# Threshold attention and a feed-forward block: where chunks are converted, when q and k are asked for, and where a slot's products end

## The chip, the cores and the metric

The kernel runs on one core of one Trainium2 chip. The time is the device time of one execution in microseconds (us). A core has five engines that run their own instruction streams and wait for each other by semaphores: TensorE (PE; its weight loads are listed apart as PEld), VectorE (DVE), ScalarE (ACT), GpSimd (POOL) and SyncE (SP), which here only issues DMAs.

## The reference

Eight batches of eight heads with 576 rows of 64 features go through an attention that keeps only the scores within tau of the row's maximum. The heads' outputs side by side are the input x (512 features) of a block with layer norm, a product to 2048 hidden features, a relu, a product back, and a residual.

```python
scores = scale * np.matmul(q, k.transpose(0, 1, 3, 2))
thresh = np.max(scores, axis=-1, keepdims=True) - tau
scores = np.where(scores >= thresh, scores, -1000000000.0)
scores = scores - np.max(scores, axis=-1, keepdims=True)
attn = np.exp(scores)
attn = attn / (np.sum(attn, axis=-1, keepdims=True) + 1e-09)
attn_out = np.matmul(attn, v)                       # (8, 8, 576, 64)
x = attn_out.transpose(0, 2, 1, 3).reshape(8, 576, 512)
xn = (x - mu) / np.sqrt(var + 1e-06) * g_ln         # mu, var over the 512 features
out = x + np.maximum(xn @ w_ch1, 0.0) @ w_ch2       # 512x2048 and 2048x512
```

q, k, v and g_ln are float32. w_ch1 and w_ch2 arrive as float64, and the kernel converts them to float32 itself.

## The kernel before

The work is cut into 72 slots, nine for each batch. A slot does the scores, exponentials and thresholding of four blocks of 128 rows. Its weights are transposed and multiplied with v one slot later. In the first batch the transposing is done on TensorE (`turn_weights`); from the second on by DVE in 32x32 blocks, a way through DRAM (`scr`) and back (`em`). Between these, a slot has four places (quarters) where products of the feed-forward block are put into TensorE's stream.

```python
for n in range(NS):
    b, s = divmod(n, SLOTS)
    ticks = (0, 2, 3) if n < 6 else range(5)      # ticks of the weights' conversion
    ...
    tick(0)
    scores(b, s)                                  # PE
    run(n, -1)
    rest = exponentials()                         # DVE maxima, ACT exponentials
    es, thr = next(rest)                          # the first two blocks
    run(n, 0)                                     # asks for em of the slot before
    conversion.fetch(2)
    run_all(stores)                               # output DMAs
    second_part(n, 0)                             # products, quarter 0
    next(rest, None)                              # the last two blocks' exponentials
    u = (n + 1) // SLOTS * HP + (n + 1) % SLOTS
    if (n + 1) % SLOTS < HP and u < len(units):
        turn(u)                                   # transposes k and q of a later slot on DVE
    run_all(aside)
    tick(1)
    run(n, 1)
    second_part(n, 1)
    weights(es, thr)                              # DVE threshold, POOL normalization
    run_all(aside)
    run_all(stores)
    tick(2)
    run(n, 2)
    second_part(n, 2)
    tick(3)
    ...  # turn_weights, or turn_blocks (DVE) and four DMAs to scr
    at_quarter(n + 1, 3, lambda b=b, s=s, box=box: values_of(b, s, box[0]))
    ...
    if (n + 1) % SLOTS < HP and u + 1 < len(units):
        load_qk(u + 1)                            # eight DMAs on SyncE, into single buffers
    run_all(aside)
    conversion.fetch(2)
    run(n, 3)                                     # mean of a group, values of the slot before
    ...  # load_v
    second_part(n, 3)
    tick(4)
    run_all(aside)
```

The feed-forward block works on groups of 288 rows, two for each batch. Its products are handed out by a generator; `second_part` takes as many as a running account (`owed`) allows, by the room of each quarter.

```python
def ffn_steps(g):
    ...
    for d in range(ND):                           # 16 feature tiles of the hidden layer
        while conversion.ended < 4 * (d // 4 + 1):
            yield 0                               # weights not there yet
        p1 = ps_ff.tile([128, TOK], F32, tag="ff", name="p1")   # tag "ff": two buffers
        for c in range(NK):                       # 4 products
            product(p1, ...)
            if c < NK - 1:
                yield 1
        nc.scalar.activation(hidden[:, d], p1, func=AF.Relu)
        yield 1
        ...  # d == 1: squares; d == 8: variance (a product into "ff"), 1/std
    for m in range(NK):
        p2 = ps_ff.tile([128, TOK], F32, tag="ff", name="p2")
        for d in range(ND):
            ...
            product(p2, ..., rhs=hidden[:, d], ...)
            if d < ND - 1:
                yield 1
        aside.append(lambda m=m, p2=p2: add_to_x(g, m, p2, rb))   # DVE product o, POOL sum
        yield 1
```

The conversion turns 32 chunks of float64 words. Each takes a piece of borrowed memory for its raw words and one for what is made of them. A piece is kept with the number of the first chunk that may no longer use it, and the tick at which it was given back.

```python
def piece(self, i, wait):
    fit = [p for p in self.free if p[0] > i and p[1] < self.ticks - wait]
    if not fit:
        return None
    got = min(fit, key=lambda p: p[0])
    ...
def fetch(self, most=99):                         # DMA of raw words, got = self.piece(i, 1)
    ...
def begin(self):
    i = self.begun
    got = self.piece(i, -1)
    if got is None:
        return
    ...  # DVE: two operations into the first half; ACT: one in place, a square into the second
def carry(self):                                  # POOL: adds, gives the raw piece back
    ...
def end(self):                                    # DVE, for w_ch1 also POOL; gives the made piece back
    ...
def tick(self):
    self.ticks += 1
    if self.ended < self.carried and self.due[self.ended] <= self.ticks:
        self.end()
    if self.carried < self.begun:
        self.carry()
    if self.begun < self.fetched:
        self.begin()
```

Of the kernel before, what the change touches and what calls it, by code (L numbers as in the profile page):

```python
# [18 lines left out]
def kernel(  # L19
# [36 lines left out]
    HP = H // 2  # L56
# [6 lines left out]
    SLOTS = 2 * HP + 1  # L63
# [28 lines left out]
    units = [(b, hp) for b in range(B) for hp in range(HP)]  # L92
    loaded, values_in, turned = {}, {}, {}

    def product(out, lhsT, rhs, **flags):


        for h in range(2):
            r = slice(64 * h, 64 * h + 64)
            nc.tensor.matmul(out[r], lhsT=lhsT[:, r], rhs=rhs, **flags)  # L100
# [59 lines left out]
    class Weights:  # L160
# [67 lines left out]

        def begin(self):
            i = self.begun  # L230
            got = self.piece(i, -1)
            if got is None:
                return
            self.made[i] = got
            a, y = got[2][:, :WC], got[2][:, WC:]
            self.begun += 1
            self.due.append(self.ticks + 3)
            au, hi = a.bitcast(U32), self.words(i, U32)[:, :, 1]
            nc.vector.tensor_scalar(
                out=au, in0=hi, scalar1=3, scalar2=0x3FFFFFFF,  # L240
                op0=ALU.logical_shift_left, op1=ALU.bitwise_and,
            )
            nc.vector.scalar_tensor_tensor(
                out=au, in0=hi, scalar=0xC0000000, in1=au,
                op0=ALU.bitwise_and, op1=ALU.bitwise_or,
            )
            nc.scalar.activation(
                self.words(i, I32)[:, :, 0], self.words(i, U32)[:, :, 0],
                func=AF.Copy, scale=2.0**-29,
            )  # L250
            nc.scalar.activation(y, self.words(i, F32)[:, :, 1], func=AF.Square)
# [34 lines left out]
    def by_blocks(u):  # L286

        return units[u][0] > 0

    def turn(u):  # L290

        q_in, k_in = loaded.pop(u)
        qT = att.tile([128, 2, QH], F32, tag="qT", bufs=4, name="qT")
        kT = att.tile([128, S], F32, tag="kT", bufs=4, name="kT")
        qd = q_diag[u % HP]  # L300
        nc.gpsimd.tensor_scalar(
            out=q_in, in0=q_in, scalar1=scl_sb, scalar2=1.0, op0=ALU.mult, op1=ALU.mult
        )
        nc.vector.transpose(kT, k_in.rearrange("p n c -> p (n c)"))  # L304
        for s in range(2):
            part = q_in[:, 9 * s : 9 * s + 8]
            if by_blocks(u):
                nc.vector.transpose(
                    qT[:, s].rearrange("p (j a c) -> p a j c", j=2, a=4),
                    part.rearrange("p (a j) c -> p a j c", j=2),  # L310
                )
            else:
                nc.vector.transpose(qT[:, s], part.rearrange("p n c -> p (n c)"))
        for h in range(2):
            r = slice(64 * h, 64 * h + 64)
            nc.vector.transpose(
                qd[r, r].rearrange("p (t c) -> p t c", t=2),
                q_in[r].rearrange("p (t n) c -> p t n c", t=2)[:, :, 8],
            )
        turned[u] = (qT, kT, qd)  # L320
# [221 lines left out]
    def run_all(calls):  # L542
        now = calls[:]
        calls.clear()
        for fn in now:
            fn()
# [23 lines left out]
    def ffn_steps(g):  # L570


        xc = centred.pop(g)
        rb = None
        for d in range(ND):
            while conversion.ended < 4 * (d // 4 + 1):
                yield 0
            p1 = ps_ff.tile([128, TOK], F32, tag="ff", name="p1")
            for c in range(NK):
                product(  # L580
                    p1, lhsT=w1_sb[c][:, d * 128 : (d + 1) * 128], rhs=xc[:, c],
                    start=(c == 0), stop=(c == NK - 1),
                )
                if c < NK - 1:
                    yield 1
            nc.scalar.activation(hidden[:, d], p1, func=AF.Relu)  # L586
            yield 1
            if d == 1:
                sq = ffn.tile([128, NK, TOK], F32, tag="sq", bufs=1, name="sq")
                nc.scalar.activation(sq, xc, func=AF.Square)  # L590
                for c in range(1, NK):
                    nc.gpsimd.tensor_tensor(out=sq[:, 0], in0=sq[:, 0], in1=sq[:, c], op=ALU.add)
            if d == 8:
                var = ps_ff.tile([128, TOK], F32, tag="ff", name="var")
                product(var, lhsT=avg_sb, rhs=sq[:, 0], start=True, stop=True)
                rb = ffn.tile([128, TOK], F32, tag="rb", bufs=2, name="rb")
                nc.scalar.activation(rb, var, func=AF.Sqrt, bias=eps_sb)  # L597
                aside.append(lambda: nc.vector.reciprocal(rb, rb))  # L598
# [4 lines that stand above are left out]
                while conversion.ended < conversion.n1 + d + 1:  # L603
                    yield 0
                product(
                    p2, lhsT=w2_sb[:, d, m * 128 : (m + 1) * 128], rhs=hidden[:, d],
                    start=(d == 0), stop=(d == ND - 1),
                )
                if d < ND - 1:
                    yield 1  # L610
            aside.append(lambda m=m, p2=p2: add_to_x(g, m, p2, rb))
            yield 1

    QUARTERS = 4
# [3 lines left out]
    queue = []  # L620
    issued = 0
    owed = 0.0
# [5 lines left out]
    def run(n, i):  # L628
        for fn, args in later_calls.pop((n, i), ()):
            fn(*args)  # L630

    def ready(g):

        b, t = divmod(g, 2)
        return QUARTERS * (b * SLOTS + (HP, 2 * HP)[t] + 2) + (2, 4)[t]

    def second_part(n, i):

        nonlocal issued, owed
        if not queue:  # L640
            return
        at = QUARTERS * n + i
        g = issued // STEPS
        left = sum(ROOM[t % QUARTERS] for t in range(at, ready(g + 1))) if g + 1 < NG else 0
        owed += ((g + 1) * STEPS - issued) * ROOM[i] / left if left > 0 else 8
        while queue and owed >= 0.5:
            got = next(queue[0], None)
            if got is None:
                queue.pop(0)
                if left > ROOM[i]:  # L650
                    break
            elif got == 0:
                owed = 0.0
                break
            else:
                issued += 1
                owed -= 1
# [21 lines left out]
    for n in range(NS):  # L679
        b, s = divmod(n, SLOTS)  # L680
        ticks = (0, 2, 3) if n < 6 else range(5)

        def tick(i):
            if i in ticks:
                conversion.tick()

        tick(0)
        scores(b, s)
        run(n, -1)
        rest = exponentials()  # L690
        es, thr = next(rest)
        run(n, 0)
        conversion.fetch(2)
        run_all(stores)
        second_part(n, 0)
        next(rest, None)

        u = (n + 1) // SLOTS * HP + (n + 1) % SLOTS
        if (n + 1) % SLOTS < HP and u < len(units):
            turn(u)  # L700
        run_all(aside)
        tick(1)
        run(n, 1)
        second_part(n, 1)
        weights(es, thr)
# [6 lines that stand above are left out]
        box = []  # L712
        if by_blocks(b * HP):
            scr = turn_blocks(s, es)
            at_quarter(n + 1, 0, lambda s=s, scr=scr, box=box: box.append(fetch(s, scr)))
        else:
            made = turn_weights(s, es)
            at_quarter(n + 1, -1, next, made)
            at_quarter(n + 1, 0, lambda made=made, box=box: box.append(next(made)))
        at_quarter(n + 1, 3, lambda b=b, s=s, box=box: values_of(b, s, box[0]))  # L720
        if s in (HP, 2 * HP):
            group_ready(2 * b + (s > HP))
        if (n + 1) % SLOTS < HP and u + 1 < len(units):
            load_qk(u + 1)
        run_all(aside)
        conversion.fetch(2)
        run(n, 3)
        if b == 0 and s < HP - 2:
            load_v(s + 2)
        elif n >= SLOTS - 2 and (n + 2) % SLOTS < HP and n < NS - 2:  # L730
            load_v((n + 2) // SLOTS * HP + (n + 2) % SLOTS)
# [3 lines that stand above are left out]
# [37 lines left out]
```

## Time and profile before

| | |
|---|---|
| time, median of 3 runs | 1594.85 us (1592.58 to 1596.5) |
| span of the profiled run | 1586.6 us, 28851 instructions |
| PE busy | 1431.7 us (90%) |
| PEld busy | 854.8 us (54%) |
| DVE busy | 835.3 us (53%) |
| POOL busy | 477.1 us (30%) |
| ACT busy | 441.8 us (28%) |
| mean granted TensorE clock | 0.959 |
| DMA | 205.07 MB, mean 129 GB/s |

The page of a profile gives such sums, a picture of the span in 40 slices, and groups of like instructions by line, engine and operation. The other views are answers to questions put to the trace: who waited for whom (engine, line, what it waited for, us in total, times, longest), the busy time of each engine in a stretch, and the instructions in order of time, where the brackets at the end of a line give the engine's idle time before it and what ended that. "x5" is a count, and an arrow points from what is read to what is written. Names are those of the tiles in the kernel, with `p` for p1 and p2 and `sc` for the score banks, in which the values are summed too; lines are those of the kernel printed above.

### The profile page before, as it was taken

The page shows a single profiled execution, that of the slowest core. Times are in us where ns is not written, and L with a number is a line of the kernel's source. Part 1 is how long each engine was busy: PE and PEld are TensorE (multiplying, and loading weights), DVE is VectorE, ACT ScalarE, POOL GpSimd, SP SyncE. Part 2 cuts the span into 40 slices and gives each one's busy share as a digit, 9 for nine tenths or more (in the row PEclk, how much of TensorE's full clock was granted, in tenths as well). Part 3 has the DMA queues.
Part 4 walks back from the last instruction along what each step waited for, and adds up shares of the span by engine and source line. Part 5 has one row for each costly group of instructions (what it writes and reads, how often), then busy time and mean ns, then how long its engine had stood idle before and what let it go on. Part 6 is the DMA issues. An engine that isn't in the chain of part 4 may idle for free.

```text
span 1586.6 us, 28851 instructions
## 1 busy us (share of the span) xinstructions
PE 1431.7 (90%) x11700; PEld 854.8 (54%) x11700; DVE 835.3 (53%) x1380; ACT 441.8 (28%) x797; POOL 477.1 (30%) x737
## 2 busy tenths in 40 slices
PE   3556789999989998999989998999989999999998
PEld 2334445665555555565546555565555655565554
DVE  4856765455464555555464545555554556545210
ACT  2445542313132231313123230323223231323120
POOL 3654532222232313222232322222232322222110
PEclk7768899999999999999999999999999999999999
DMA  9610217654675556755565556745575556645300
GB/s 213 170 54 27 61 37 167 148 132 132 153 155 154 131 139 148 178 130 133 131 163 136 146 133 151 168 124 141 137 156 148 142 134 152 158 129 137 100 9 16
DMA packets 460693, 205.07 MB, mean 129 GB/s; under 512 B 275024, under 2 KB 420176, under 8 KB 460560
## 3 DMA queue, kind: packets, MB, share of 16 engines
q1 hardware_dynamic: 458160, 202.93, 52.2%
q8 instruction: 92, 1.51, 0.4%
q10 hardware_dynamic: 2368, 0.30, 0.2%
q14 instruction: 41, 0.34, 0.1%
q0 software_dynamic: 32, 0.00, 0.0%
HBM read 119.41 MB, written 83.76 MB: 128 GB/s over the span
## 4 chain that ended last, share of the span: by engine, by line
PE 64%; DVE 8%; SPq 8%; DMA 6%; issue 5%; ACT 4%; POOL 4%; POOLq 0%; ACTq 0%; DVEq 0%
PE p L100 45%; PE sc L492 9%; PE sc L359 7%; SPq L112 5%; DMA em<-scr 4%; DVE neg L372 3%; ACT e L383 3%; POOL e L395 2%; DVE e L389 2%; PE sc L100 2%; SPq L459 2%; ACT hidden L586 1%; SPq L126 1%; SPq L130 1%; DVE et L453 1%
## 5 line engine op out<-in xcount | busy, mean ns | idle before, releaser
L100 PE MATMUL p<-xc,w 128*64 128x288 f32 x4096 | 521.2, 409 | 26.3 <-ACT hidden L586 24.2
L100 PE MATMUL p<-hidden,w 128*64 128x288 f32 x4096 | 515.7, 408 | 0.0
L100 PEld LDWEIGHTS p<-xc,w 128*64 128x64 f32 x4096 | 293.5, 137 | 232.7 <-ACT hidden L586 43.8
L100 PEld LDWEIGHTS p<-hidden,w 128*64 128x64 f32 x4096 | 298.8, 138 | 192.5 <-issue 2.7
L372 DVE TENSOR_REDUCE neg<-sc 128x2 f32<-128x1152 f32 x144 | 189.4, 1353 | 315.3 <-PE sc L359 252.4
L395 POOL TENSOR_SCALAR e<-e,den 128x576 f32<-128x576 f32 x288 | 219.4, 779 | 332.8 <-DVE den L393 300.8
L383 ACT ACTIVATE e<-sc,neg 128x576 f32<-128x576 f32 x288 | 194.0, 743 | 278.4 <-DVE neg L372 278.2
L389 DVE SCALAR_TENSOR_TENSOR e<-sc,thr,e 128x576 f32<-128x576 f32 x288 | 220.0, 813 | 33.7 <-ACT e L383 33.4
L359 PE MATMUL sc<-kT,qT 64*128 64x512 f32 (+3 forms) x1024 | 161.0, 454 | 41.8 <-ACT x L509 11.6
L453 DVE STREAM_TRANSPOSE et<-e 128x1152 f32<-128x1152 f32 x112 | 153.1, 1372 | 71.7 <-POOL e L395 63.7
L586 ACT ACTIVATE hidden<-p 128x288 f32<-128x288 f32 x256 | 103.3, 414 | 253.9 <-PE p L100 253.7
L492 PE MATMUL sc<-em,v_in 128*64 128x256 f32 (+1 forms) x1536 | 154.1, 347 | 16.4 <-DMA em<-scr 11.3
L359 PEld LDWEIGHTS sc<-kT,qT 64*128 64x128 f32 x1024 | 89.4, 198 | 128.3 <-issue 79.5
L376 POOL TENSOR_SCALAR thr<-neg,low_sb 128x2 f32<-128x2 f32 x144 | 39.2, 272 | 363.9 <-DVE neg L372 362.9
L492 PEld LDWEIGHTS sc<-em,v_in 128*64 128x64 f32 x1536 | 101.9, 145 | 63.7 <-issue 19.5
L509 ACT COPY x<-sc 128x256 f32<-128x256 f32 x64 | 23.8, 372 | 355.6 <-PE sc L492 342.4
L551 POOL TENSOR_TENSOR o<-o,x 128x288 f32<-128x288 f32 x64 | 51.0, 796 | 138.8 <-DVE o L550 138.4
L550 DVE TENSOR_TENSOR o<-p,rb 128x288 f32<-128x288 f32 x64 | 28.1, 439 | 109.3 <-PE p L100 109.1
L304 DVE STREAM_TRANSPOSE kT<-k_in 128x576 f32<-128x576 f32 x32 | 24.8, 775 | 83.6 <-DMA k_in<-in_k_dram 79.7
L518 POOL TENSOR_TENSOR sum<-sum,x 128x256 f32<-128x256 f32 (+1 forms) x64 | 31.9, 498 | 104.6 <-ACT x L509 99.7
L416 PE MATMUL tp<-ident,e 128*128 128x128 f32 x144 | 26.7, 334 | 28.9 <-ACT em L423 28.5
L598 DVE RECIPROCAL rb<-rb 128x288 f32<-128x288 f32 x16 | 31.3, 1954 | 39.4 <-ACT rb L597 39.4
(93 smaller groups left out, 700.7 us busy)
## 6 DMA issues: line engine op xcount, KB each, us to landing
scr<-et SPq DMA_DIRECT2D x252, 288.0 KB, 4.9
em<-scr SPq DMA_DIRECT2D x63, 1024.0 KB, 5.9
q_in<-in_q_dram SPq DMA_DIRECT2D x128, 72.0 KB, 3.4
out_dram<-ot SPq DMA_DIRECT2D x256, 36.0 KB, 4.3
k_in<-in_k_dram SPq DMA_DIRECT2D x124, 72.0 KB, 2.6
v_in<-in_v_dram SPq DMA_DIRECT2D x64, 128.0 KB, 2.8
rest<-scr SPq DMA_DIRECT2D x63, 128.0 KB, 5.8
w<-in_moe_w_ch_dram SPq DMA_DIRECT2D x13, 512.0 KB, 4.9
```

Source lines behind the costliest of these rows:

```text
L100: nc.tensor.matmul(out[r], lhsT=lhsT[:, r], rhs=rhs, **flags)
L112: (engines[i] if engines else nc.sync).dma_start(out=t[32 * g : 32 * g + 32], in_=src[b, 2 * hp + h, :, 32 * e : 32 * e + 32].rearrange("( ...
L359: nc.tensor.matmul(sc[h][:, at : at + n], lhsT=qT[r, half, j * 128 : (j + 1) * 128], rhs=kT[r, o : o + n], start=True, stop=True,)
L372: nc.vector.tensor_reduce(out=neg[:, i], in_=sc[h][:, : 2 * S].rearrange("p (j n) -> p j n", j=2), axis=AXL.X, op=ALU.max, negate=True,)
L376: nc.gpsimd.tensor_scalar(out=thr[:, i], in0=neg[:, i], scalar1=-1.0, scalar2=low_sb, op0=ALU.mult, op1=ALU.add,)
L383: nc.scalar.activation(es[:, i], blocks[i], func=AF.Exp, bias=neg[:, i : i + 1])
L389: nc.vector.scalar_tensor_tensor(out=es[:, i], in0=blocks[i], scalar=thr[:, i : i + 1], in1=es[:, i], op0=ALU.is_ge, op1=ALU.mult, accum_o ...
L395: nc.gpsimd.tensor_scalar(out=es[:, i], in0=es[:, i], scalar1=den[:, i : i + 1], scalar2=1.0, op0=ALU.mult, op1=ALU.mult,)
L453: nc.vector.transpose(et[:, :, 64 * h : 64 * h + 64].rearrange("p n (j c) -> p j n c", j=2), es[:, 2 * h : 2 * h + 2].rearrange("p j (n c) ...
L492: nc.tensor.matmul(dst[64 * h : 64 * h + 64], lhsT=vt[:, c, h, :] if c < J else vr[:, h, :], rhs=pick(em[:, c] if c < J else er, hp, h), s ...
L551: nc.gpsimd.tensor_tensor(out=o, in0=o, in1=groups[g][:, m], op=ALU.add)
L586: nc.scalar.activation(hidden[:, d], p1, func=AF.Relu)
```

## The change

Three things change. A chunk of the conversion now takes, for what is made of its words, a piece that has been free for two ticks or more, and one just given back only if there is none. The loads of q and k are asked for right behind the turning that empties their buffers, in front of the output stores and of the writes to `scr`, where they were behind both. And in the last quarter of a slot the products go on until a feature tile of the hidden layer is complete, so that its relu can run before the next slot's exponentials.

```diff
         def begin(self):
             i = self.begun
-            got = self.piece(i, -1)
+            got = self.piece(i, 1) or self.piece(i, -1)
...
             nc.scalar.activation(hidden[:, d], p1, func=AF.Relu)
-            yield 1
+            yield 2
...
                 if d < ND - 1:
-                    yield 1
+                    yield 2
             aside.append(lambda m=m, p2=p2: add_to_x(g, m, p2, rb))
-            yield 1
+            yield 2
...
         owed += ((g + 1) * STEPS - issued) * ROOM[i] / left if left > 0 else 8
-        while queue and owed >= 0.5:
+        got = 2
+        while queue and (owed >= 0.5 or got == 1 and i == QUARTERS - 1):
             got = next(queue[0], None)
...
             turn(u)
+            if u + 1 < len(units):
+                load_qk(u + 1)
         run_all(aside)
...
-        if (n + 1) % SLOTS < HP and u + 1 < len(units):
-            load_qk(u + 1)
         run_all(aside)
         conversion.fetch(2)
```

## The prediction

> **What bounds the kernel now.** I call one pass of the outer loop a slot (n = 0 to 71), its four parts q0 to q3, and write s for n mod 9, the place in a batch. I read the busy slices first, then two stretches.
>
> ```profile
> PE   3556789999989998999989998999989999999998
> ...
> PEclk7768899999999999999999999999999999999999
> ```
>
> ```profile
> 0.00:244.70 244.70, 151.76 (x984) 93.21 (x984) 155.49 (x250) 103.21 (x180) 119.42 (x147) 0.78 0.38 96
> 244.70:1586.60 1341.90, 1279.98 (x10718) 761.54 (x10716) 679.82 (x1130) 338.57 (x617) 357.71 (x590) 0.99 0.56 135
> ```
>
> The columns are the stretch, its length, then busy PE, weight loads, DVE, ACT, POOL, then clock, DMA share and GB/s. Up to 244.7 us (slots 0 to 9, in which the weights are converted) TensorE idles 244.7 - 151.8 = 92.9 us and is granted 0.78 of its clock. Afterwards it idles 1341.9 - 1280.0 = 61.9 us in 1342. So the second stretch is bound by TensorE, and only its gaps can be won; the first is bound by something else. The waits of TensorE over the whole span say what the gaps are:
>
> ```profile
> PE tp L416 <- ACT em L423: 28.5, 13, 6.9
> PE p L100 <- ACT hidden L586: 24.2, 28, 1.5
> PE mean L100 <- DVE o L550: 19.3, 6, 4.2
> ...
> PE sc L359 <- ACT x L509: 11.6, 3, 7.4
> PE sc L492 <- DMA em<-scr: 11.3, 10, 2.4
> ...
> PE sc L359 <- ACT x L500: 10.2, 1, 10.2
> ```
>
> (Total, times, longest.) Placing each gap by its time, the waits on em L423 and on x (L509, L500) lie in the first stretch. Those on hidden, o and em<-scr lie in the second and repeat in every batch: the mean waits for o in slots with s = 1, em<-scr mostly for s = 0, 1, 2, the relus (hidden) for s = 2, 3, 7, 8 with 0.5, 0.8, 0.7 and 1.5 us. There is one hidden cost. Two slots with s = 1:
>
> ```profile
> 601.70:627.40 25.70, 22.28 (x158) 12.98 (x156) 12.88 (x25) 3.01 (x5) 5.00 (x9) 0.87 0.71 161
> ...
> 1146.00:1168.10 22.10, 19.33 (x158) 11.85 (x156) 12.83 (x25) 3.00 (x5) 4.96 (x9) 1.00 0.70 159
> ```
>
> The same 158 matmuls take 22.28 us at clock 0.87 and 19.33 at 1.00. In the first the wait for o was 3.42 us long, in the second 2.77. The other two of this kind above 3.4 us (3.43 and 4.22) end in clock 0.93 and 0.87 as well.
>
> Why is o late? In the timeline of one such slot, that of SyncE, DVE and PE:
>
> ```profile
> 965.29 5.49 SPq L112 DMA_DIRECT2D q_in<-in_q_dram  x4
> 970.82 2.40 SPq L112 DMA_DIRECT2D k_in<-in_k_dram  x4
> ...
> 975.64 0.53 SPq L468 DMA_DIRECT2D em<-scr  x1
> ```
>
> ```profile
> 975.22 0.78 DVE L304 STREAM_TRANSPOSE kT<-k_in 128x576 f32<-128x576 f32 x1 [6.88 <-DMA k_in<-in_k_dram]
> ```
>
> ```profile
> 981.14 1.23 PE L100 MATMUL mean<-sum,avg_sb 128*64 128x288 f32 x4 [4.22 <-DVE o L550]
> ```
>
> The loads of q and k are asked for behind the four writes of scr (961.37 to 965.19), so DVE stands 6.88 us before it can turn k. Its thresholding, the product o behind that, and et and scr all come late; TensorE waits for o, and in the next slot for em. The eight q and k issues also hold SyncE for 7.9 us in front of the fetch of em. Loading is thus a loop of its own that runs slower than TensorE where s = 0, 1, 2.
>
> **What the Trainium skill says.** "PSUM — Partial Sum Buffer", section "Engine vs sequencer instructions": the queues of ScalarE, VectorE and GpSimd are strict FIFO. The 6.88 us agree: thresholds whose scores were long there wait behind the turning. "TensorE: Matmul & The Clock Gate", Part 1: the clock gate falls back after an idle window of about 3.4 us. The trace agrees: 3.42 us of idling was followed by clock 0.87, 2.77 by 1.00. "SBUF — State Buffer", section "Who interferes with whom": a DVE instruction with two SBUF inputs contends with GpSimd's reads; so DVE and POOL freed of mutual waits overlap at a price. The DVE lines of the conversion vary a lot here (L239 0.43 to 1.51 us), which fits, though its cause isn't shown.
>
> **The change part by part.**
>
> Part 1, the pieces of the conversion. A chunk began in the piece with the shortest life, often freed at the same tick by a POOL operation that had hardly been queued. Two of the waits this makes, on DVE and ACT:
>
> ```profile
> 97.10 0.43 DVE L239 TENSOR_SCALAR w<-et 128x512 uint32<-128x512 uint32 x1 [3.75 <-POOL w L257]
> ```
>
> ```profile
> 137.24 0.67 ACT L251 ACTIVATE w<-w 128x512 f32<-128x512 f32 x1 [7.03 <-POOL w L257]
> ```
>
> The first stands in front of slot 4's maximum, the second in front of the copy x that the scores of slot 6 wait for. Counting the pieces through by the rule of the code: before, 22 of the 32 chunks begin in a piece freed at the same tick or one earlier; after, none do, and no chunk lacks a piece. The price: in the code's order the fetches of chunks 20 to 30 slip by up to a slot, and the last chunk ends at the fourth tick of slot 9 instead of the third, which moves 8 products from slot 9 to slot 10. Slot 9 has 24.3 us with 20.9 of PE, so that costs nothing.
>
> The gain by slots: slot 4 (27.8 us), 3.75 of DVE's wait plus most of the 7.44 us in which the scores of slot 5 wait for x, about 8; slot 5 (24.1), most of the 10.23 in which those of slot 6 wait, about 7; slots 0 to 3, which hold ACT waits on POOL of this kind too, about 4; slots 7 and 8 about 3, since the waits there are for operations on POOL that remain (L266 on the carry) and for em copies behind the exponentials. Sum 22. POOL and DVE will then overlap more and slow each other, so I take 18, with 5 to 30 possible.
>
> Part 2, the loads of q and k. Nothing is removed: 8 issues per unit move from behind the writes of scr to behind the turning. A slot with s = 8, where k is loaded long before, shows the result: turning from +5.0 to +7.3 us, et done at +15.0. With that pattern in s = 0, 1, 2: q and k issued from +7.3 on, at 0.5 to 1.0 us each, are landed by about +17, and the next turning wants them at +24. The last write of scr lands 7.8 us after the first is issued (939.64 to 947.43); so, with the shortest s = 0 slot of the trace (764.2 to 782.3), em is issued 15.0 + 7.8 - 18.1 = 4.7 us into the next slot and lands 6 later at 10.7, where TensorE wants it after 13 to 14. The product o comes at about +11, the mean is wanted at 2.3 + 22 x 0.485 = 13.0 (2.3 us of scores; 0.485 us is one product, 7.98 us for 64 matmuls at 4 a product less the lead-in; by the pacing rule 22 products lie ahead). So both waits vanish: 19.3 + 11.3 = 30.6 us, and with them the slow clock: the four s = 1 slots with PE busy 22.28, 20.87, 22.08 and 20.92 go to 19.33 or less, 8.8 us. Sum 39.
>
> Part 3, ends with a feature tile. No instruction is added or lost. In q3 up to three more products run, and q0 has as many fewer. I went through the four places with relu waits (PSUM holds two tiles, so tile d+2 waits for the relu of d, and ACT does the exponentials of the slot first: two from +3.9 to +5.25, all four until +6.5). s = 7: 0.70 to 0. s = 2: unchanged, 0.5. s = 8: tile 11 now ends in q0 or q1; its relu comes at 6.8 or 8.1 and TensorE wants it at 6.2: 1.49 to 0.6-2.0. s = 3: tile 8 and the variance fill TensorE only until +4.9, while the relu of 8 comes behind all exponentials at +6.9: 0.76 to 2.0. Per batch 3.46 becomes 3.2 to 4.5; over eight batches +2 to -8 us. I take 0: the wait moves, it does not go.
>
> Sum: 18 + 39 + 0 = 57, and 2 for a first stretch that reaches the full clock sooner. 1594.85 - 59 = 1536, rounded to 1535.
>
> **Rivals.** (a) SyncE becomes the bound for s = 1, 2: it runs strictly in order, and q and k now stand ahead of four output stores and of scr. Per slot: em and rest 1.0, eight stores 4.4 to 5.8, q and k 4.2 to 7.9, scr 3.8, v 2.3, the wait for scr 1.7: 17.4 to 22.5, against a slot of 19.1. At the upper end em is again 2 to 4 us late twice a batch, 20 to 30 us given back: about 1560. For it speaks that q took 5.49 us here; against it that this was behind scr, with its writes in flight, and the k issues took 0.5 each. (b) The q and k transfers collide with em: DMA share is only 0.7 there, and em is issued first; at most 1 us on a margin of 2.3. (c) The first stretch gives nothing, because the waits moved from POOL to fetches now asked for late: 1555. (d) Part 3 really removes its 24 us: 1512.
>
> **Range and chances.** (a) and (c) together give about 1578, only then is 2% (1563) missed. Range 1512 to 1562. Faster 0.86, same 0.11, slower 0.03.
>
> **What would show it.** Right: k_in no longer a wait of DVE (79.7 us now), mean and em<-scr gone from TensorE's waits, s = 1 slots at clock 1.00 and about 19 us, the first ten slots near 225 us, waits on hidden still 20 to 30 us with more of them at s = 3. Wrong: em<-scr waits at s = 2, 3 behind SyncE (rival a), waits of L239 or L247 on weight DMAs (c), waits on hidden gone (d).

## The result and the profile after

The changed kernel takes 1528.93 us (median of 4 runs, 1528.43 to 1529.49) where the kernel before takes 1593.71 us (4 runs beside them, 1589.87 to 1596.5). The ratio is 0.9595, with a 95% interval of 0.9574 to 0.9617: 64.8 us less, against the 60 predicted (1535), inside the range of 1512 to 1562. Lines after 570 stand one lower in the changed kernel: the relu, L586 before, is L587.

First the sums and two rows of the busy slices on the page of the changed kernel; the columns are those of the page before.

```profile
PE 1416.8 (93%) x11700; PEld 833.7 (55%) x11700; DVE 837.7 (55%) x1380; ACT 442.2 (29%) x797; POOL 487.7 (32%) x737
...
PE   3557899999999999999999999999999999999998
...
PEclk8777899999999999999999999999999999999999
```

The row of PE, which held eights along its whole length, now shows nines from the sixth slice to the last but one. TensorE is busy for 14.9 us less (1431.7 before) with the same 11700 matmuls; fewer of them run at half the clock.

I cut both spans at the start of slot 11, where both kernels have done the same 1156 matmuls by the trace. That is 265.8 us before and 248.2 us after. The stretches of the changed kernel (columns as in the prediction: stretch, length, busy PE, weight loads, DVE, ACT, POOL, clock, DMA share, GB/s):

```profile
0.00:248.20 248.20, 167.78 (x1156) 101.33 (x1156) 171.47 (x276) 104.54 (x185) 134.80 (x156) 0.82 0.45 110
248.20:1527.70 1279.50, 1249.04 (x10546) 732.36 (x10544) 666.23 (x1104) 337.63 (x612) 352.91 (x581) 0.99 0.57 139
```

Cut at the same place, the kernel before has:

```profile
0.00:265.80 265.80, 172.86 (x1156) 105.63 (x1157) 168.85 (x276) 106.22 (x185) 125.14 (x156) 0.80 0.40 100
265.80:1586.60 1320.80, 1258.88 (x10546) 749.12 (x10544) 666.45 (x1104) 335.56 (x612) 351.99 (x581) 0.99 0.55 135
```

So 17.6 us were won up to slot 11 and 41.3 after it. Of those 41.3, the idle time of TensorE gives 31.5 (1320.80 - 1258.88 = 61.92 against 1279.50 - 1249.04 = 30.46) and its busy time 9.8. In the clock's record, half speed behind slot 11 (without the last 5 us) falls from 20.5 us to 10.2; half of that difference, 5.1 us, is an estimate of what the clock has in the 9.8, and the rest isn't placed. In the first stretch POOL is busy for 134.80 us instead of 125.14 with the same 156 instructions, a price of the kind that the prediction took off.

The waits of TensorE in the changed kernel (in all, times, longest):

```profile
PE tr L429 <- ACT em L423: 32.4, 8, 6.1
PE p L100 <- ACT hidden L587: 23.6, 21, 2.0
```

The rows of the mean and of em<-scr are gone. The relus (hidden) still cost 23.6 us where they cost 24.2, but in 21 waits instead of 28, and the longest is 2.0 instead of 1.5: they moved, as predicted. The waits for the copy em (L423) that lead the list lie in the first stretch. DVE's waits for k_in, 79.7 us in 21 before, are one of 4.8 us.

A slot with s = 1 (it begins at 925.0) in the order of SyncE's issues:

```profile
930.28 0.45 SPq L468 DMA_DIRECT2D em<-scr  x1
...
934.99 2.06 SPq L112 DMA_DIRECT2D q_in<-in_q_dram  x4
937.09 2.12 SPq L112 DMA_DIRECT2D k_in<-in_k_dram  x4
939.31 1.95 SPq L563 DMA_DIRECT2D out_dram<-ot  x4
941.35 3.89 SPq L459 DMA_DIRECT2D scr<-et  x4
```

Four of the eight output stores still go out ahead of q and k. Next come the turning and the mean of the same slot, each from its engine's timeline:

```profile
929.97 0.77 DVE L304 STREAM_TRANSPOSE kT<-k_in 128x576 f32<-128x576 f32 x1
```

```profile
938.96 0.66 PE L100 MATMUL mean<-sum,avg_sb 128*64 128x288 f32 x4
```

Neither carries brackets: the turning finds k there at +5.0 us, and the mean follows the products ahead of it without a gap. em is issued at +5.3 us. The eight issues take 4.2 us; ahead of the change they took 7.9 in such a slot.

### The profile page after: what moved, and what is told of

It is laid out like the page before. It is cut to its first block, busy times and chain, and to the rows that moved or that the text cites. A ratio compares the mean times of both kernels' runs of the same rounds, so it can differ in the third digit from the quotient of the medians.

```text
span 1527.7 us, 28886 instructions
## 1 busy us (share of the span) xinstructions
PE 1416.8 (93%) x11700; PEld 833.7 (55%) x11700; DVE 837.7 (55%) x1380; ACT 442.2 (29%) x797; POOL 487.7 (32%) x737
## 4 chain that ended last, share of the span: by engine, by line
PE 83%; ACT 5%; DVE 5%; POOL 2%; issue 2%; SPq 1%; DMA 1%; POOLq 0%; ACTq 0%; DVEq 0%
PE p L100 62%; PE sc L492 10%; PE sc L359 8%; ACT e L383 4%; DVE neg L372 3%; PE sc L100 2%; POOL e L395 1%; DVE e L389 1%; SPq L112 1%; ACT hidden L587 1%; PE mean L100 1%; ACT L383 0%; DMA v_rest<-in_v_dram 0%; ACT em L423 0%; PE tr L429 0%
## 5 line engine op out<-in xcount | busy, mean ns | idle before, releaser
L100 PE MATMUL p<-xc,w 128*64 128x288 f32 x4096 | 528.5, 414 | 24.9 <-ACT hidden L587 23.6
L100 PEld LDWEIGHTS p<-hidden,w 128*64 128x64 f32 x4096 | 291.2, 137 | 198.4 <-issue 1.4
L395 POOL TENSOR_SCALAR e<-e,den 128x576 f32<-128x576 f32 x288 | 227.3, 806 | 282.9 <-DVE den L393 263.1
L389 DVE SCALAR_TENSOR_TENSOR e<-sc,thr,e 128x576 f32<-128x576 f32 x288 | 219.1, 813 | 26.7 <-ACT e L383 26.2
L587 ACT ACTIVATE hidden<-p 128x288 f32<-128x288 f32 x256 | 105.1, 415 | 278.2 <-PE p L100 276.1
L359 PE MATMUL sc<-kT,qT 64*128 64x512 f32 (+3 forms) x1024 | 154.3, 439 | 22.7 <-DVE e L389 10.9
L492 PE MATMUL sc<-em,v_in 128*64 128x256 f32 (+1 forms) x1536 | 149.1, 340 | 4.8 <-DVE e L389 4.4
L359 PEld LDWEIGHTS sc<-kT,qT 64*128 64x128 f32 x1024 | 86.1, 191 | 106.2 <-issue 79.9
L492 PEld LDWEIGHTS sc<-em,v_in 128*64 128x64 f32 x1536 | 97.4, 144 | 49.2 <-DVE e L389 7.1
L593 POOL TENSOR_TENSOR sq<-sq 128x288 f32<-128x288 f32 x48 | 38.7, 807 | 45.8 <-ACT sq L591 43.3
L492 PE MATMUL sc<-rest,v_rest 128*64 128x256 f32 (+1 forms) x384 | 49.3, 336 | 0.0
```

The costliest lines, as they stand in the source:

```text
L359: nc.tensor.matmul(sc[h][:, at : at + n], lhsT=qT[r, half, j * 128 : (j + 1) * 128], rhs=kT[r, o : o + n], start=True, stop=True,)
L389: nc.vector.scalar_tensor_tensor(out=es[:, i], in0=blocks[i], scalar=thr[:, i : i + 1], in1=es[:, i], op0=ALU.is_ge, op1=ALU.mult, accum_o ...
L395: nc.gpsimd.tensor_scalar(out=es[:, i], in0=es[:, i], scalar1=den[:, i : i + 1], scalar2=1.0, op0=ALU.mult, op1=ALU.mult,)
L492: nc.tensor.matmul(dst[64 * h : 64 * h + 64], lhsT=vt[:, c, h, :] if c < J else vr[:, h, :], rhs=pick(em[:, c] if c < J else er, hp, h), s ...
```

## The experiments

All ratios are to the kernel before on the same chip, with 95% intervals.

### Each part alone, and parts 1 and 2 together

e1: part 1 alone.

```diff
-            got = self.piece(i, -1)
+            got = self.piece(i, 1) or self.piece(i, -1)
```

> Part 1 alone on the kernel before. My theory: the first ten slots get shorter because DVE and ACT no longer wait for POOL's operation of the same tick; slot 11 begins some 17 us earlier than before (265.8 us) and the second stretch keeps all its gaps (mean waits 19 us, em 11 us, hidden 24 us): 1594 - 17 = 1577, 1570 to 1583. Rival: the first stretch gets shorter only together with the earlier loads of q and k, then under 8 us here (over 1586).

Measured: 1578.92 us, ratio 0.9922 (0.9909 to 0.9935), 11.8 us less. The starts of the slots show where. At slot 6 it stands at 119.5 us instead of 138.3: 18.8 won in slots 0 to 5, where the prediction's terms sum to 19. From there to slot 11, 6.9 are given back (253.9 against 265.8). Slot 6 alone takes 26.5 us instead of 20.1. Two lines from it, of ACT and of PE:

```profile
125.18 0.67 ACT L251 ACTIVATE w<-stage 128x512 f32<-128x512 f32 x1 [5.09 <-POOL w L257]
125.75 1.05 ACT L423 COPY em<-tp 128x512 f32<-128x512 f32 x2
```

```profile
126.46 1.94 PE L416 MATMUL tp<-ident,e 128*128 128x128 f32 x8 [3.57 <-ACT em L423]
```

ACT waits 5.09 us for POOL, with the copy em behind it in its queue, and TensorE waits 3.57 us for that copy. POOL has become the engine that the chunks wait for. Slot 6 in the kernel before and in e1:

```profile
138.30:158.40 20.10, 17.41 (x118) 11.48 (x118) 16.12 (x28) 12.94 (x23) 10.87 (x15) 0.87 0.08 27
```

```profile
119.50:146.10 26.60, 19.02 (x118) 11.52 (x118) 21.34 (x32) 12.91 (x23) 22.01 (x26) 0.74 0.18 60
```

POOL has 26 instructions in slot 6 instead of 15, and 28 instead of 36 in slots 4 and 5: work of those slots has moved into slot 6, where POOL is now busy for 22.0 of 26.6 us. Its instructions also take longer. These are the 44 normalizations in the first 262 us, of the kernel before and then of e1 (busy us and mean ns of one behind the first bar):

```profile
L395 POOL TENSOR_SCALAR e<-e,den 128x576 f32<-128x576 f32 x44 | 42.3, 976 | 62.9 <-DVE den L393 52.3 <-PE sc L492 10.6
```

```profile
L395 POOL TENSOR_SCALAR e<-e,den 128x576 f32<-128x576 f32 x44 | 49.5, 1138 | 68.3 <-DVE den L393 57.7 <-PE sc L492 10.6
```

One takes 162 ns more, 7.2 us in all. The Trainium skill, "SBUF — State Buffer", section "Who interferes with whom", has DVE instructions with two SBUF inputs contend with GpSimd's reads; that fits, and a slower POOL is measured here, but no run separates this cause from another. (L239, which the prediction names for it, reads one input, w<-et; L243 and L266 read two, and all three vary.)

e2: part 2 alone (the loads behind the turning).

```diff
             turn(u)
+            if u + 1 < len(units):
+                load_qk(u + 1)
...
-        if (n + 1) % SLOTS < HP and u + 1 < len(units):
-            load_qk(u + 1)
```

> Part 2 alone. My theory: DVE waits on k_in fall from 80 to about 10 us, mean and em<-scr leave TensorE's waits, no slot with s = 1 falls to the slow clock; first stretch unchanged, hidden waits as before (24 us): 1594 - 39 = 1555, 1548 to 1561. Rival (SyncE becomes the bound behind q, k and the stores): em<-scr waits of 2 to 4 us at s = 2, 3 and 1575 or more.

Measured: 1546.07 us, ratio 0.9714 (0.9699 to 0.9729), 44.6 us less, all of it behind slot 11:

```profile
267.50:1544.39 1276.89, 1245.76 (x10546) 730.48 (x10544) 667.09 (x1104) 335.58 (x612) 351.77 (x581) 1.00 0.57 139
```

Idle time falls to 31.1 us, by 30.8: the two waits that vanish were put at 19.3 + 11.3 = 30.6. Busy time falls by 13.1 us. The clock's record shows no half speed from slot 11 to the last 5 us; before, there were 20.5 us of it. The slots s = 0, 1, 2 take 18.1, 19.1 and 19.4 us in every batch from the fourth on (18.6, 18.6 and 19.4 in the third).

e3: part 3 alone (ends with a feature tile).

```diff
-            yield 1
+            yield 2
...
-        while queue and owed >= 0.5:
+        got = 2
+        while queue and (owed >= 0.5 or got == 1 and i == QUARTERS - 1):
```

> Part 3 alone. My theory: the waits on hidden move from s = 7, 8 to s = 3 and stay 20 to 28 us in sum: 1592 to 1600, no gain. Rival (the relus before the exponentials really free TensorE): waits on hidden under 8 us and 1575 or less.

Measured: 1600.34 us, ratio 1.0051 (1.0032 to 1.0070): 9.6 us more. TensorE's waits in e3:

```profile
PE sc L492 <- DMA em<-scr: 24.7, 14, 3.5
...
PE mean L100 <- DVE o L550: 12.3, 6, 3.1
```

em costs 13.4 us more, the mean 7.0 less, the relus (22.2) 2.0 less. Half speed behind slot 11 grows from 20.5 to 34.1 us, some 6.8 us of work more. Together +11.2, where that stretch grew by 11.0 (1592.0 - 260.2 = 1331.8 against 1320.8). The slots fit that: s = 8 shrinks from 20.3 us to 18.4 in five of six batches, and 9.1 of the 13.4 us lie in the slot behind it (s = 0). With the loads still late, TensorE comes to em sooner and has to wait there. The traced execution was the fastest of six (1593.79 us; the others 1596.98 to 1602.66) and reached slot 11 5.6 us earlier than the kernel before, so it shows 5.4 of the 9.6 us.

e4: parts 1 and 2 without part 3 (the diffs of e1 and e2).

> The changed kernel without part 3 (parts 1 and 2). In the trace of the changed kernel the 1.97 us waits at s = 3 are followed in three of seven batches by 3.4 us at half the clock. My theory: without part 3 the waits at s = 3 are 0.8 us as before and the clock stays up, waits on hidden 24 us: 1525, that is 1521 to 1530, 0 to 8 us faster than the changed kernel (1529). Rival: part 3 was worth something once the other waits are gone: 1535 or more.

Measured: 1531.59 us, ratio 0.9625 (0.9609 to 0.9642), 59.1 us less, near 11.8 + 44.6 = 56.4. The three parts alone sum to 46.8 and together give 64.8. So part 3 loses nothing beside parts 1 and 2; the intervals of e4 and of the changed kernel overlap, and its gain there is near the noise. That the loss needs the late loads fits the waits for em in e3; parts 2 and 3 without part 1 were not run. Beside the other two parts it gives 3.6 us up to slot 11 (251.8 to 248.2) and takes 2.6 behind it (1276.9 to 1279.5), by these two profiles.

e11 is the changed kernel once more, run beside e12 further down, to see how far executions of one program scatter.

> The changed kernel itself, as the yardstick for the next one on the same chip: 0.9595 of the kernel before.

Measured: 1528.36 us, ratio 0.9600 (0.9577 to 0.9624). Slot 11 begins at 245.7 instead of 248.2, and the rest takes 1279.4 instead of 1279.5. The first stretch scatters by some 2.5 us between executions of one program, the rest hardly. The 3.6 us for part 3 in the first stretch is therefore rough.

### Where the loads may stand

e5: the loads later. In the kernel before, from slot 9 on, behind the fetch of em in the slot that follows.

```diff
-            load_qk(u + 1)
+            if n < SLOTS:
+                load_qk(u + 1)
+            else:
+                at_quarter(n + 1, 0, load_qk, u + 1)
```

> The kernel before, but from slot 9 on q and k are asked for behind the next slot's fetch of em. SyncE then no longer holds em back, while k comes later. My theory (the late turning is the root, the place in front of em a minor part): DVE's waits on k_in grow from 80 to 130 us or more, o and em stay late, TensorE's mean and em waits stay above 30 us in sum: 1590 or slower. Rival (the 7.9 us of issues in front of em are the root): em<-scr waits go, mean waits stay, 1575 to 1585.

Measured: 1715.09 us, ratio 1.0778 (1.0755 to 1.0801), 122.6 us more. SyncE and DVE there:

```profile
619.18 0.45 SPq L468 DMA_DIRECT2D em<-scr  x1
...
620.24 3.23 SPq L112 DMA_DIRECT2D q_in<-in_q_dram  x4
623.51 3.43 SPq L112 DMA_DIRECT2D k_in<-in_k_dram  x4
```

```profile
629.84 0.78 DVE L304 STREAM_TRANSPOSE kT<-k_in 128x576 f32<-128x576 f32 x1 [9.70 <-DMA k_in<-in_k_dram]
```

DVE stands 9.70 us for k, and 220.0 us in 21 waits over the whole span (79.7 before). TensorE waits 64.9 us for o and 60.9 for e (L389). em is issued first here, at +4.1 us (the slot begins at 615.1), and TensorE's waits for em<-scr are gone, 11.3 us before: to that extent SyncE's order was in em's way. But e and o are now late, because the turning holds DVE. Half speed behind slot 11 grows from 20.5 to 122.9 us, so part of the 122.6 us is the clock. This shows the direction of the cause: the time hangs on when k lands, far more than on SyncE's place for em.

e6: part 2 with the loads behind the second output stores, still ahead of scr.

```diff
         run_all(stores)
+        if (n + 1) % SLOTS < HP and u + 1 < len(units):
+            load_qk(u + 1)
         tick(2)
```

> The kernel before with the loads moved only half the way: behind the second group of output stores, still in front of the writes of scr. My theory (what counts is that they do not stand behind scr, whose first write waits for et): within 3 us of part 2 alone (1546). Rival (they must also stand in front of the stores): 1555 or more, with DVE waits on k_in above 20 us.

Measured: 1545.42 us, ratio 0.9705 (0.9690 to 0.9719), the same as e2. In slot 46 the loads land at +18.2 us instead of +16.2, and the next turning wants them at about +24. Being ahead of scr is what counts; the margin is several us.

### Why the pieces helped

e9: part 1 with a piece that has been free for one tick instead of two.

```diff
-            got = self.piece(i, 1) or self.piece(i, -1)
+            got = self.piece(i, 0) or self.piece(i, -1)
```

> A smaller dose of part 1 alone: a chunk begins in a piece that has been free for one tick or more, instead of two, and takes one of the same tick only if there is none. If the waits on pieces just given back are what part 1 saves, the gain lies between none and that of part 1 alone (1579): 1580 to 1588, with waits of DVE L239 and ACT L251 on POOL and DVE between those of the two (before: L239 on POOL 32 us, part 1 alone: none). Rival (the gain comes from the order of the fetches, whatever the waits): no relation, 1590 or under 1577.

Measured: 1588.48 us, ratio 0.9945 (0.9926 to 0.9964), between the kernel before and e1 by its middle; its interval overlaps e1's. By the rule of the code 17 chunks still begin in a piece given back one tick earlier, none in one of the same tick. The longest row of ACT's waits for the carries on POOL in e9:

```profile
ACT w L251 <- POOL w L257: 13.7, 2, 6.9
```

The same row is 20.7 us in the kernel before and 5.1 in e1. Taken over all rows, DVE's waits of L239 for POOL are 31.7 us before, 18.6 in e9 and none in e1, ACT's waits of L251 for POOL 39.7, 37.9 and 19.9. Slot 6 begins at 122.9 (119.5 in e1, 138.3 before), slot 11 at 260.2 (253.9, 265.8). Both sums lie between those of the other two kernels, as they should if a chunk waits for POOL's queue behind the tick in which its piece was given back, though ACT's hardly fall with one tick.

### The relu waits that are left

These three change only how products are dealt out. ROOM is the room of the four quarters.

e7: parts 1 and 2, and more products early in a slot.

```diff
-    ROOM = (0.6, 1.0, 1.0, 0.6)
+    ROOM = (1.0, 1.0, 0.6, 0.6)
```

> Parts 1 and 2 (no part 3) with the rooms of the quarters 1.0, 1.0, 0.6, 0.6 instead of 0.6, 1.0, 1.0, 0.6: the first quarter gets 8 to 9 products, so two relus come between the two pairs of exponentials instead of behind both. If relus standing behind the exponentials in ACT's order are the cause of the waits on hidden, these fall from 24 to about 16 us and the time from 1531 to 1522. Rival: the waits on hidden stay, or the later second pair of exponentials makes o and em late again: 1531 or more.

Measured: 1522.5 us, ratio 0.9560 (0.9546 to 0.9575), 9.1 us below e4. The waits on hidden are 15.8 us.

e8: the same edit in the changed kernel, with part 3.

> The changed kernel with the same rooms (1.0, 1.0, 0.6, 0.6). By the same reasoning the wait at s = 3 falls from 1.97 to about 0.9 us and no half-clock window follows it: hidden waits about 16 us, 1516, that is 1511 to 1522. Rival: no change (1529).

Measured: 1518.27 us, ratio 0.9536 (0.9521 to 0.9550): the shortest time of all runs, some 10 us below the changed kernel and 4.2 below e7, beside which it ran. So part 3 pays here. A slot with s = 3 in the changed kernel and then in e8, ACT first:

```profile
794.32 2.64 ACT L383 ACTIVATE e<-sc,neg 128x576 f32<-128x576 f32 x4 [3.29 <-DVE neg L372]
796.83 0.43 ACT L587 ACTIVATE hidden<-p 128x288 f32<-128x288 f32 x1
```

```profile
797.31 9.19 PE L100 MATMUL p<-xc,w 128*64 128x288 f32 x60 [1.97 <-ACT hidden L587]
```

```profile
444.54 1.37 ACT L383 ACTIVATE e<-sc,neg 128x576 f32<-128x576 f32 x2 [3.29 <-DVE neg L372]
445.80 0.41 ACT L587 ACTIVATE hidden<-p 128x288 f32<-128x288 f32 x1
```

```profile
446.26 4.10 PE L100 MATMUL p<-xc,w 128*64 128x288 f32 x32 [0.70 <-ACT hidden L587]
```

In the changed kernel quarter 0 ends before a tile does, so the program puts all four exponentials ahead of the relu, and TensorE waits 1.97 us. In e8 the larger room lets quarter 0 reach the end of the tile, the relu stands behind two exponentials, and the wait is 0.70; a second one of 0.70 follows in the slot. Waits on hidden fall from 23.6 us to 16.5, none above 0.7, and no half speed is left between slot 11 and the last 5 us (10.2 us in the changed kernel).

e10: e8 without the rule that ends a quarter when a group's products are done.

```diff
                 queue.pop(0)
-                if left > ROOM[i]:
-                    break
```

> The changed kernel with rooms 1.0, 1.0, 0.6, 0.6, and a new group's products begin in the quarter in which its turn comes, instead of the one after it (the account loses no quarter when a group's products are out). At s = 2 the first two relus then come between the pairs of exponentials: the 0.51 us at s = 2 go and the two of 0.70 with them, waits on hidden 16 to about 8 us: 1512, that is 1507 to 1517. Rival: the product waits for the centred values instead (a wait on xc at s = 2 of 1 us or more): 1518 or slower.

Measured: 1522.6 us, ratio 0.9527 (0.9505 to 0.9549), no clear difference from e8. The waits on hidden halve again, to 8.1 us, but others grow:

```profile
PE sc L492 <- DVE e L389: 10.3, 9, 2.2
```

It was 4.4 us in e8. By these traces the stretch behind slot 11 is 1270.2 us against 1269.2, and slot 11 began later (251.9 against 247.5). A miss: most of what left one wait came back in another.

e12: the changed kernel with part 3 only in the slots before 11.

```diff
-        while queue and (owed >= 0.5 or got == 1 and i == QUARTERS - 1):
+        while queue and (owed >= 0.5 or got == 1 and i == QUARTERS - 1 and n < SLOTS + 2):
```

> The changed kernel with part 3 only in slots 0 to 10. From the traces, part 3 brings slot 11 forward by 3.6 us (251.8 to 248.2) and costs 2.6 us after it, in which the half-clock windows behind the 1.97 us waits have 5 us. My theory: the early part is kept and the later part is saved, 1 to 5 us faster than the changed kernel, with waits of 0.8 us at s = 3 and no half-clock window after slot 11. Rival: both differences are chance of the two executions, no difference (within 1 us).

Measured: 1525.06 us (1524.71 to 1526.72), ratio 0.9578 (0.9555 to 0.9602), beside e11 with 1528.36 (1526.85 to 1529.75). The waits on hidden are 24.3 us in 28, as before the change, and yet the stretch behind slot 11 is 2.2 us shorter than in e11 (1277.2 against 1279.4): e12 has no half speed there, e11 has 10.2 us of it. All slots with s = 3 take 19.6 us. What part 3 costs behind slot 11 is thus the clock, not the waits: half of the 10.2 us, 5.1, is more than the 2.2 lost.

## Why the prediction was right, by its steps

- **What bounds the kernel.** Right: 31.5 of the 41.3 us won behind slot 11 are gaps of TensorE, and the first stretch was bound by the conversion, where e1 alone won 18.8 us in slots 0 to 5.
- **Part 1, 18 us.** It gave 11.8 alone and 14.5 beside part 2 (1546.07 to 1531.59). In e1, slots 0 to 3 give 4.5 us (about 4 was put down), slot 4 9.7 (8) and slots 7 and 8 2.1 (3). Slot 5 gives 4.5 instead of 7: the scores of slot 6 wait 0.5 us for x instead of 10.2, but TensorE waits 8.2 us for the copy em (L418) instead of 1.9. The term that was missing is slot 6: it takes 6.5 us more, with the chunks now waiting for POOL. The 4 us taken off for POOL and DVE slowing each other were a cost of that kind, and too small. "Costs nothing" for the products moved from slot 9 to slot 10 held in the changed kernel (45.1 us for both slots, 45.4 before). In e1 the two take 2.5 more, of which 2.1 are waits for o, which the late loads make. Slot 10 begins at 223.3 us in the changed kernel ("near 225").
- **Part 2, 39 us.** The idle terms, 30.6, measured 30.8. The times inside a slot with s = 1 came as worked out: em issued at +5.3 (4.7), q and k landed at +16.0 ("about +17"). The clock term, 8.8, was too small: busy time fell by 13.1. It was taken from four slots alone; half of the 20.5 us of half speed behind slot 11 is 10.3, and the other 2.8 are not placed.
- **Part 3, 0 us.** The waits: s = 7 to 0 as put down, s = 2 unchanged at 0.51, s = 8 from 1.49 to 0.52 in five batches and 1.79 in two (0.6 to 2.0), s = 3 from 0.76 to 1.97 (2.0). Together 3.4 per batch instead of 3.46. That it is +9.6 alone, and a small gain beside parts 1 and 2, was not foreseen; nor was the half speed behind the waits at s = 3.
- **The sum.** Part 1 alone fell short by 6, part 2 alone gave 6 more, and part 3 alone lost 10: that the total came within 5 is partly luck. The 2 us for the clock of the first stretch were not separated.
- **The rivals.** (a) fell: TensorE has no wait for em<-scr left; the eight issues take 4.2 us, their lower end. (b) fell: em was issued 0.6 us later than worked out, and nothing waits for it. (c) fell: L239 waits for a weight's DMA once, for 1.2 us (1.1 before), L247 for 7.3 us as before. The largest loss against the 18.8 us of slots 0 to 5, 6.5 us in slot 6, is the waits for POOL. (d) fell: waits on hidden are 23.6 us of 24.2.

## What to carry to other kernels

When one load is asked for in a queue that runs in order, its place behind slow writes can cost more than its length: eight issues moved ahead of four writes were worth 44.6 us, and moved behind the next fetch they cost 122.6. A resource picked as the one with the shortest life is often the one just given back by an engine with a queue; give it a tick or two, and look then at the engine that the wait moves to. A change that only shortens a slot can pay only when what follows is already there, so try it again once the late transfer has been mended.

## What the runs showed of the hardware

An idle time of 1.97 us was followed by half speed. Two stretches of the changed kernel, the first with such a wait in it, at n = 30:

```profile
620.50:623.90 3.40, 1.43 (x14) 0.69 (x12) 3.10 (x8) 3.38 (x6) 0.27 (x1) 0.99 0.33 85
623.90:627.30 3.40, 3.40 (x18) 1.75 (x16) 3.31 (x5) 1.07 (x3) 2.65 (x4) 0.50 0.94 336
```

The wait of the same length one batch earlier, at n = 21, in stretches that lie on the same grid:

```profile
446.40:449.80 3.40, 1.64 (x14) 0.72 (x10) 3.10 (x5) 2.78 (x5) 0.54 (x2) 1.00 0.39 98
449.80:453.20 3.40, 3.19 (x26) 1.92 (x28) 3.31 (x8) 2.35 (x4) 1.35 (x2) 1.00 0.91 296
```

1.43 us of busy time in a stretch of 3.40 is followed by a clock of 0.50, 1.64 us by 1.00. In the clock's record the times of half speed begin on one grid of 3.413 us and last one or more of its cells. I counted the full-speed cells behind slot 11 in the kernel before, e1, e3 and the changed kernel: of the 24 in which TensorE was busy for 0.43 or less of the time, 23 were followed by half speed; of those with 0.446 or more, none. The idle time alone doesn't decide: the 2.77 us of the prediction fell on two cells, in which TensorE was busy for two thirds and for half of the time, while the 2.88 us of the slot with clock 0.93 that begins at 1325.2, the shortest wait of the prediction's four, fell almost wholly into one cell (busy for 0.18) and were followed by half speed.

Both runs of the changed kernel show it at the same three of seven places (n = 30, 39, 48). The prediction leaned on the Trainium skill, "TensorE: Matmul & The Clock Gate", Part 1, for an idle window of about 3.4 us; the length of the window agrees, but it doesn't have to be idle, only busy for less than some 0.44 of the time in these runs. What such a cell costs on top of the gap is 1.7 us by estimate (half of 3.413). The slots s = 3 and 4 of the changed kernel take 40.7 us together in the three batches with half speed behind the wait and 39.0 in the other four.
